# Diagonal 16x16 blocks of a chunk inverse moved from TensorE to GpSimd

## Chip, core and metric

The kernel runs on one core of one Trainium2 chip. The metric is device time in microseconds (us), from the first to the last instruction of a launch with what the device adds around it. PE is TensorE, PEld its weight loads, DVE is VectorE, ACT is ScalarE, POOL is GpSimd, SP is SyncE, which here only issues DMAs.

## What is computed

A delta rule attention (4 batches, 8 heads, 768 positions, head dimension 48) feeds a mixture of 8 experts that keeps at most 80 tokens of each expert (model dimension 384, hidden 1024). All in f32.

```python
for t in range(S):                                   # attention, per batch and head
    y[:, :, t] = einsum('bhd,bhde->bhe', q[:, :, t], state)
    v_old = einsum('bhde,bhd->bhe', state, kt)        # kt: normalised key
    state = state + bt * einsum('bhd,bhe->bhde', kt, vt - v_old)
...
expert_idx = argmax(x @ w_gate, axis=1)               # x: attention output, (3072, 384)
for e in range(8):
    tok_idx = the 80 tokens of expert e with the largest gate weight
    out[tok_idx] = gate_w[tok_idx, None] * (relu(x[tok_idx] @ w1[e]) @ w2[e])
```

## The kernel before

The sequence is cut into 12 chunks of 64 positions (`NC`, `C`). All 32 heads of a chunk are worked on at once: two halves `e` of the partitions times two `p` times eight `g`. A chunk has two parts. `prep(c)` (lines 304 to 377) doesn't need the state of earlier chunks: it transposes the keys and queries (L311, copied by ACT at L314), forms the two 64x64 Gram matrices (L319), scales and masks them into `B1` and `PT` (L324, L327, and POOL's affine selects at L330 and L332), and builds the inverse of the unit triangular 64x64 matrix `B1` of each head by six doublings: blocks of 2 come from the masks (L336, L340, L343), then five levels each multiply on PE (L353), mask on DVE (L357), multiply twice (L362 and L370) and copy on ACT (L366, L374). The result is `Y`. `chain(c)` (lines 384 to 448) is the recurrent part: state times keys and queries (L393, L398), `R` (L396), `Y` times `R` (L406), `U` (L409), the new state (L415, L419), the output rows `x` (L423, L428), which go to `x_rows` in DRAM (L433), and the gate logits (L439 to L447). `gate(b)` turns the logits of three chunks into expert choices and candidate lists (`cand`), mostly in small DVE instructions.

Each f32 matmul stands twice in the trace, as two instructions with a weight load each, so a group of 32 heads is 64 rows of PE; the 128x128 transposes stand once. One chunk has, by the loops of the code, 16 transposes (L311), 128 of L319, 64 of L340, 320 of L353, 256 of L362, 320 of L370, and 338 of the chain (five groups of 64, 6 of L439, 12 of L446): 1442.

`weave` alternates the steps of `chain(c)`, of the second half of `prep(c + 1)` and of the first half of `prep(c + 2)`; engines run their instructions in the order of one static list each. PSUM tiles of two banks (`mtile`) are used in turn, three of them. `norms(c)` is a square on ACT (L240), some twelve small DVE instructions, and one POOL multiply (L258).

Two of ten weight buffers are loaded early (`WR0 = 2`); the other eight loads stand right behind the chunk loop (L564 and L565), and behind them on SP the six loads of `mg` (L588), a gather of the candidate lists over partitions. Then a selection on DVE and PE finds the tokens (L593 to L647), POOL gathers them from `x_rows` (L659), and the experts run on PE (L683, L691).

Of the kernel before, what the change touches and what calls it, by code (L numbers as in the profile page):

```python
# [24 lines left out]
def kernel(  # L25
# [20 lines left out]

    nc = tc.nc
# [4 lines left out]
    C = 64  # L52
# [18 lines left out]

    const = ctx.enter_context(tc.tile_pool(name="const", bufs=1))
# [11 lines left out]
    eye = const.tile([128, 64], F32, name="eye")  # L84
    nc.gpsimd.memset(strict, 1.0)
    nc.gpsimd.memset(eye, 0.0)
    for e in range(2):
# [6 lines left out]
    widths = []  # L94
    w = 1
    while w < C:
        widths.append(w)
        w *= 2
    masks = []
    for w in widths:  # L100
        m = const.tile([128, 64], F32, name=f"mask{w}")
        nb = 64 // (2 * w)
        nc.gpsimd.memset(m, 0.0)
        for e in range(2):
            r = slice(64 * e, 64 * e + 64)
            lo = m[r].rearrange("p (g j) -> p g j", g=nb)[:, :, 0:w]
            nc.gpsimd.memset(lo, -1.0)
            nc.gpsimd.affine_select(out=lo, in_=lo, compare_op=Alu.is_ge, fill=0.0, base=-w,
                                    pattern=[[-2 * w, nb], [0, w]], channel_multiplier=1)
            nc.gpsimd.affine_select(out=lo, in_=lo, compare_op=Alu.is_ge, fill=0.0, base=2 * w - 1,  # L110
                                    pattern=[[2 * w, nb], [0, w]], channel_multiplier=-1)
        nc.gpsimd.tensor_tensor(out=m, in0=m, in1=eye, op=Alu.add)
        masks.append(m)
    mask1T = const.tile([128, 64], F32, name="mask1T")
    nc.gpsimd.memset(mask1T, 0.0)
    for e in range(2):
        r = slice(64 * e, 64 * e + 64)
        odd = mask1T[r].rearrange("p (g j) -> p g j", j=2)[:, :, 1:2]
        nc.gpsimd.memset(odd, -1.0)
        nc.gpsimd.affine_select(out=odd, in_=odd, compare_op=Alu.is_equal, fill=0.0, base=0,  # L120
                                pattern=[[-2, 32], [0, 1]], channel_multiplier=1)
    nc.gpsimd.tensor_tensor(out=mask1T, in0=mask1T, in1=eye, op=Alu.add)
# [25 lines left out]
    WR0, WR = 2, 10  # L148
    w_t, w_pools = {}, [wpool]

    def load_w(i):
# [4 lines left out]
        w_t[i] = w_pools[late].tile([128, nch, DK * F // nch], F32, name=f"w{i}", tag="w", bufs=WR - WR0 if late else WR0)  # L156
        nc.sync.dma_start(w_t[i], src[i // 2].rearrange("(c p) f -> p c f", p=128))

    with ExitStack() as actx:
# [13 lines left out]
        NKB, NQB = 4, 3  # L173
# [3 lines left out]
        def load_k(c):  # L177
            if c >= NC:
                return
            kr[c] = inp.tile([128, NB, D], F32, name="kr", bufs=4)  # L180
# [29 lines left out]
        for t in kn + qn:  # L210
            nc.vector.memset(t[:, :, D:], 0.0)
        load_q(0)
        load_k(1)
        load_v(0)
        load_q(1)
        load_k(2)
# [85 lines left out]
        Fs = {}  # L302

        def prep(c):
            kb, qb = kn[c % NKB], qn[c % NQB]
            KT = mat.tile([128, NQ, 128], F32, name="KT")
            QT = mat.tile([128, NQ, 128], F32, name="QT")
            for dst, src in ((KT, kb), (QT, qb)):
# [6 lines left out]
            yield  # L315
            pk, pq = mtile(), mtile()
            for ps, r in ((pk, KT), (pq, QT)):
# [4 lines left out]
            B1 = mat.tile([128, 2, NQ, 64], F32, name="B1")  # L322
            PT = mat.tile([128, 2, NQ, 64], F32, name="PT")
            halves(lambda s: nc.vector.tensor_tensor(  # L324
                out=B1[:, :, s], in0=sq4(pk)[:, :, s],
                in1=beta_t[:, c, :, s].unsqueeze(3).to_broadcast([128, 2, 4, 64]), op=Alu.mult))
            halves(lambda s: nc.vector.tensor_tensor(out=PT[:, :, s], in0=sq4(pq)[:, :, s], in1=wide(strict), op=Alu.mult))  # L327
            bv = B1.rearrange("r p g w -> r (p g) w")
            for e in range(2):
                nc.gpsimd.affine_select(out=bv[hs(e)], in_=bv[hs(e)], compare_op=Alu.is_gt, fill=0.0, base=0,  # L330
                                        pattern=[[0, 2 * NQ], [1, 64]], channel_multiplier=-1)
                nc.gpsimd.affine_select(out=bv[hs(e)], in_=bv[hs(e)], compare_op=Alu.not_equal, fill=1.0, base=0,  # L332
                                        pattern=[[0, 2 * NQ], [1, 64]], channel_multiplier=-1)
            yield
            Y = mat.tile([128, 2, NQ, 64], F32, name="Y")
            nc.gpsimd.tensor_tensor(out=Y.rearrange("r p g w -> r (p g) w"), in0=bv,  # L336
                                    in1=mask1T.unsqueeze(1).to_broadcast([128, 2 * NQ, 64]), op=Alu.mult)
            px = mtile()
            tiles(lambda e, p: (e, e),
                  lambda e, p, g: nc.tensor.matmul(px[hs(e), p, 64 * g : 64 * g + 64],  # L340
                                                   lhsT=B1[hs(e), p, g], rhs=eye[hs(e)], start=True, stop=True))
            X = mat.tile([128, 2, NQ, 64], F32, name="X", bufs=2)
# [380 lines left out]
```

## Time and profile before

| | us |
|---|---|
| median of three runs | 738.8 (735.47 to 745.18) |
| the profiled execution | 735.01 |
| its span, first to last instruction | 733.3 |
| PE busy | 505.5 (69%) |
| DVE busy | 297.4 (41%) |
| ACT busy | 174.5 (24%) |
| POOL busy | 140.8 (19%) |

Busy time is the time in which at least one instruction of the engine ran. Matmuls of different quadrants of the array overlap, so many instructions of 0.2 us fit in a busy microsecond. A wait named "issue" is idle time of an engine in which it waited for nothing that the profile shows.

### The profile page before, as it was taken

To read this page: it belongs to the slowest core of one execution; us is meant where nothing else is said; L and a number is where in the kernel's file an instruction comes from. 1 tells how busy PE (TensorE), PEld (TensorE's weight loads), DVE (VectorE), ACT (ScalarE), POOL (GpSimd) and SP (SyncE) were. 2 spreads that over 40 slices of the span, in tenths; PEclk is the share of its full clock that TensorE was granted. 3 is DMA by queue.
4 is the path that set the end of the run, shared out by engine and by line. 5 is a ranking of instruction groups with operands and counts; after the bars stand their busy time and mean duration, and the time that the engine had idled before them with its cause. 6 is when DMAs were issued, how large, how long until landed. Compare 5 with 4: busy or idle time off the path is not lost. (4 is left out here: it accounts for less than half of the span.)

```text
span 733.3 us, 37473 instructions
## 1 busy us (share of the span) xinstructions
PE 505.5 (69%) x17681; PEld 456.2 (62%) x17681; DVE 297.4 (41%) x745; ACT 174.5 (24%) x326; POOL 140.8 (19%) x198
## 2 busy tenths in 40 slices
PE   0567578767786685968878677786857200499997
PEld 0557568767785675958777576786757200377774
DVE  1575356234372446324433641443363617400000
ACT  0303432323333223231322314133222000000000
POOL 7180003040310402104131040312000200301000
PEclk9969989999899999998789999899999655589999
DMA  4994033120222202121120111100001890158200
GB/s 89 265 205 122 4 75 126 34 61 4 47 47 47 48 4 46 26 47 26 22 50 5 26 26 26 25 4 11 20 5 26 308 389 13 41 189 294 74 14 14
DMA packets 94154, 53.26 MB, mean 73 GB/s; under 512 B 77616, under 2 KB 88880, under 8 KB 94000
## 3 DMA queue, kind: packets, MB, share of 16 engines
q1 hardware_dynamic: 92064, 48.78, 24.8%
q8 instruction: 139, 2.28, 1.3%
q0 software_dynamic: 768, 1.97, 0.9%
q10 hardware_dynamic: 1168, 0.11, 0.1%
q14 instruction: 15, 0.12, 0.1%
HBM read 40.42 MB, written 10.42 MB: 69 GB/s over the span
## 5 line engine op out<-in xcount | busy, mean ns | idle before, releaser
L357 DVE TENSOR_TENSOR P<-pm,mask 128x512 f32<-128x512 f32 x120 | 77.1, 684 | 111.8 <-PE pm L353 111.7
L353 PE MATMUL pm<-X,B 64*64 64x64 f32 x3840 | 93.9, 230 | 28.4 <-issue 28.4
L366 ACT COPY X<-pm 128x512 f32<-128x512 f32 x96 | 51.5, 589 | 232.3 <-PE pm L362 232.3
L353 PEld LDWEIGHTS pm<-X,B 64*64 64x64 f32 x3840 | 83.8, 143 | 32.5 <-issue 32.3
L370 PE MATMUL pm<-Y,P 64*64 64x64 f32 x3840 | 87.4, 223 | 20.1 <-issue 18.3
L370 PEld LDWEIGHTS pm<-Y,P 64*64 64x64 f32 x3840 | 79.7, 138 | 23.0 <-issue 22.9
L362 PE MATMUL pm<-P,Y 64*64 64x64 f32 x3072 | 76.6, 228 | 23.6 <-DVE P L357 11.2
L362 PEld LDWEIGHTS pm<-P,Y 64*64 64x64 f32 x3072 | 69.5, 141 | 29.0 <-issue 22.9
L330 POOL TENSOR_SCALAR_AFFINE_SELECT B<-B 64x1024 f32<-64x1024 f32 x24 | 27.5, 1147 | 287.1 <-DVE B L324 276.9
L374 ACT COPY Y<-pm 128x512 f32<-128x512 f32 x120 | 64.7, 595 | 38.9 <-PE pm L370 38.9
L683 PEld LDWEIGHTS hp<-xTe,w 128*128 128x128 f32 x384 | 49.0, 210 | 2.1 <-issue 1.2
L683 PE MATMUL hp<-xTe,w 128*128 128x80 f32 x384 | 48.8, 292 | 0.0
L691 PE MATMUL yp<-w,hT 128*80 128x384 f32 x128 | 43.4, 493 | 0.0
L686 ACT ACTIVATE hT<-hp 128x320 f32<-128x320 f32 x16 | 7.0, 438 | 149.6 <-issue 75.8
L340 PE MATMUL pm<-eye,B 64*64 64x64 f32 x768 | 32.9, 249 | 9.7 <-POOL B L332 5.7
L340 PEld LDWEIGHTS pm<-eye,B 64*64 64x64 f32 x768 | 30.8, 163 | 11.2 <-POOL B L332 8.5
L324 DVE TENSOR_TENSOR B<-pm,beta_t 128x512 f32<-128x512 f32 x24 | 15.4, 686 | 40.3 <-PE pm L319 40.3
L691 PEld LDWEIGHTS yp<-w,hT 128*80 128x80 f32 x128 | 18.9, 153 | 19.8 <-issue 19.8
L336 POOL TENSOR_TENSOR Y<-B,mask1T 128x1024 f32<-128x1024 f32 x12 | 28.3, 2362 | 0.3
L258 POOL TENSOR_TENSOR kn<-kr,inv 128x768 f32<-128x768 f32 x12 | 17.7, 1478 | 54.8 <-PE S_ps L415 38.7
L601 PE MATMUL tb_ps<-ident,thrw 8*128 8x8 f32 x1 | 0.2, 239 | 40.4 <-DVE thrw L599 40.4
L332 POOL TENSOR_SCALAR_AFFINE_SELECT B<-B 64x1024 f32<-64x1024 f32 x24 | 27.5, 1147 | 1.6
(156 smaller groups left out, 644.9 us busy)
## 6 DMA issues: line engine op xcount, KB each, us to landing
w<-in_moe_w_dram SPq DMA_DIRECT2D x16, 1536.0 KB
kr<-in_k_dram SPq DMA_DIRECT2D x24, 192.0 KB
qn<-in_q_dram SPq DMA_DIRECT2D x24, 192.0 KB
vin<-in_v_dram SPq DMA_DIRECT2D x48, 96.0 KB
out_dram<-zero SPq DMA_DIRECT2D x12, 384.0 KB
x_rows<-x SPq DMA_DIRECT2D x24, 192.0 KB
bt<-in_beta_dram ACTq DMA_DIRECT2D x32, 3.0 KB
xg<-x_rows,idx_g POOLq DMA_INDIRECT x8, 2.7
```

What stands on the lines that cost most here:

```text
L330: nc.gpsimd.affine_select(out=bv[hs(e)], in_=bv[hs(e)], compare_op=Alu.is_gt, fill=0.0, base=0, pattern=[[0, 2 * NQ], [1, 64]], channel_mu ...
L332: nc.gpsimd.affine_select(out=bv[hs(e)], in_=bv[hs(e)], compare_op=Alu.not_equal, fill=1.0, base=0, pattern=[[0, 2 * NQ], [1, 64]], channe ...
L336: nc.gpsimd.tensor_tensor(out=Y.rearrange("r p g w -> r (p g) w"), in0=bv, in1=mask1T.unsqueeze(1).to_broadcast([128, 2 * NQ, 64]), op=Alu ...
L340: lambda e, p, g: nc.tensor.matmul(px[hs(e), p, 64 * g : 64 * g + 64], lhsT=B1[hs(e), p, g], rhs=eye[hs(e)], start=True, stop=True))
L353: lambda e, p, g: nc.tensor.matmul(pp[hs(f(e, p)), pb(e, p), 64 * g : 64 * g + 64], lhsT=B1[hs(e), p, g], rhs=X[hs(e), xb(e, p), g], start ...
L357: halves(lambda s: nc.vector.tensor_tensor(out=P2[:, :, s], in0=sq4(pp)[:, :, s], in1=wide(masks[n]), op=Alu.mult))
L362: lambda e, p, g: nc.tensor.matmul(px[hs(e), xo(e, p), 64 * g : 64 * g + 64], lhsT=Y[hs(f(e, p)), yb(e, p), g], rhs=P2[hs(f(e, p)), pb(e, ...
L366: halves(lambda s: nc.scalar.copy(X[:, :, s], sq4(px)[:, :, s]))
L370: lambda e, p, g: nc.tensor.matmul(py[hs(yh(e, p)), yo(e, p), 64 * g : 64 * g + 64], lhsT=P2[hs(f(e, p)), pb(e, p), g], rhs=Y[hs(f(e, p)), ...
L374: halves(lambda s: nc.scalar.copy(Y[:, :, s], sq4(py)[:, :, s]))
L683: nc.tensor.matmul(hp[:, (f - f0) * cap : (f - f0 + 1) * cap], lhsT=w1_t[:, c, f * 128 : (f + 1) * 128], rhs=xTs[e][:, c, :], start=(c == ...
L691: nc.tensor.matmul(yp[:cap, :DM], lhsT=hT[:, f, :], rhs=w2_t[:, f, :], start=(f == 0), stop=(f == FK - 1))
```

## The change

The doubling now starts at blocks of 16. The four diagonal 16x16 blocks of each of the 32 heads are 128 small triangular systems. After `gram(c)` two DMAs write `B1` to a DRAM scratch, one DMA reads the 128 diagonal blocks back with one block per partition (`NT`), POOL inverts them by 14 steps of two instructions (`solve`), one DMA writes the 128 inverses to DRAM, and eight DMAs read them back into the block diagonal of `xe`. PE then makes the two upper merges, 16 to 32 and 32 to 64 (`merge`). `B1` gets its sign and strict triangle from a precomputed product of beta and a mask (`bm`, one POOL multiply of 128x1024), so POOL's affine selects and the multiply at L336 go. `weave` is replaced by a written order over four chunks in flight: in turn c the chain of c, the merge of c+1, the solve of c+2, and the transposes and Gram matrices of c+3. All ten weight loads now stand behind the loads of `mg`. The copy at L441 moves from DVE to ACT. Buffers of `qn` go from three to two, of `kr` from four to three.

```diff
+    PB = 16 * 65
+    a_dram = [nc.dram_tensor(f"a_blocks{i}", (128 * PB,), F32, kind="Internal") for i in range(2)]
+    i_dram = [nc.dram_tensor(f"inv_blocks{i}", (128, 256), F32, kind="Internal") for i in range(2)]
...
-    WR0, WR = 2, 10
+    WR0, WR = 0, 10
...
+        def scale(c):
+            if c >= NC:
+                return
+            norms(c)
+            bm = mat.tile([128, 2, NQ, 64], F32, name="bm", bufs=1)
+            nc.gpsimd.tensor_tensor(out=bm.rearrange("r p g w -> r (p g) w"),
+                                    in0=beta_t[:, c].rearrange("r p g -> r (p g)").unsqueeze(2).to_broadcast([128, NB, 64]),
+                                    in1=neg_strict.unsqueeze(1).to_broadcast([128, NB, 64]), op=Alu.mult)
+            bms[c] = bm
...
+            halves(lambda s: nc.vector.tensor_tensor(out=B1[:, :, s], in0=sq4(pk)[:, :, s], in1=bm[:, :, s], op=Alu.mult))
             halves(lambda s: nc.vector.tensor_tensor(out=PT[:, :, s], in0=sq4(pq)[:, :, s], in1=wide(strict), op=Alu.mult))
...
+            ad = a_dram[c % 2]
             for e in range(2):
+                dst = ad.rearrange("(e g z) -> e g z", e=2, g=NB)[e, :, : 64 * 64].rearrange("g (r w) -> r g w", w=64)
+                nc.sync.dma_start(dst, B1[hs(e)].rearrange("r p g w -> r (p g) w"))
+            NT = NTs[c] = sml.tile([128, 16, 16], F32, name="NT")
+            nc.sync.dma_start(NT, ad.rearrange("(s z) -> s z", z=PB)[:, :1024].rearrange("s (r w) -> s r w", w=64)[:, :, :16])
+
+        def solve(c):
+            if c >= NC:
+                return
+            NT = NTs.pop(c)
+            X = sml.tile([128, 16, 16], F32, name="Xs")
+            nc.gpsimd.tensor_tensor(out=X, in0=NT.rearrange("p s t -> p t s"), in1=eye16, op=Alu.add)
+            for t in range(14, 0, -1):
+                sh = [128, 15 - t, t]
+                tmp = sml.tile([128, 64], F32, name="tmp")
+                tv = tmp[:, : (15 - t) * t].rearrange("p (c s) -> p c s", s=t)
+                nc.gpsimd.tensor_tensor(out=tv, in0=X[:, t + 1 :, t : t + 1].to_broadcast(sh),
+                                        in1=NT[:, 0:t, t].unsqueeze(1).to_broadcast(sh), op=Alu.mult)
+                nc.gpsimd.tensor_tensor(out=X[:, t + 1 :, 0:t], in0=X[:, t + 1 :, 0:t], in1=tv, op=Alu.add)
+            nc.sync.dma_start(i_dram[c % 2][:, :], X.rearrange("p c s -> p (c s)"))
+            src = i_dram[c % 2].rearrange("(e g i) (c s) -> e i c g s", e=2, i=4, s=16)
+            dst = xe[c % 2].rearrange("r p g w -> r (p g) w")
+            for e in range(2):
+                for i in range(4):
+                    nc.sync.dma_start(dst[64 * e + 16 * i : 64 * e + 16 * i + 16, :, 16 * i : 16 * i + 16], src[e, i])
+
+        def merge(c):
...
+            X, B1 = xe[c % 2], B1s.pop(c)
+            py, pp = mtile(), mtile()
+            tiles(lambda e, p: (e, p),
+                  lambda e, p, g: nc.tensor.matmul(py[hs(p), e, 64 * g : 64 * g + 64], lhsT=X[hs(e), p, g], rhs=eye[hs(e)],
+                                                   start=True, stop=True))
...
+            for n in range(2):
+                nc.tensor.matmul(pp[:, n, :], lhsT=identb, rhs=eyes.rearrange("r g w -> r (g w)"), start=True, stop=False,
+                                 skip_group_check=True)
...
-            nc.vector.tensor_copy(xT, pt[:, :, : DK * 128].rearrange("r b (j w) -> r b j w", w=128))
+            nc.scalar.copy(xT, pt[:, :, : DK * 128].rearrange("r b (j w) -> r b j w", w=128))
...
-            weave(*gens)
+            load_k(c + 4)
+            load_v(c + 2)
+            ch, mg = chain(c), merge(c + 1)
+            if c > 0:
+                step(ch)
+            if c + 3 < NC:
+                trans(c + 3)
+            load_q(c + 4)
+            step(ch)
+            step(mg)
+            step(ch)
+            if c + 3 < NC:
+                gram(c + 3)
+            solve(c + 2)
+            scale(c + 4)
+            step(mg)
+            step(ch)
+            step(mg)
+            step(ch)
+            step(mg)
...
-    for i in range(WR0, WR):
-        load_w(i)
...
         for t in range(NT):
             nc.sync.dma_start(mg[:, t, :], last[t * E : (t + 1) * E, :CW])
+        for i in range(WR0, WR):
+            load_w(i)
```

The merge of a chunk is six groups of 64 instructions on PE (a transpose of `X` by the identity, `B1` times `X`, then two products of the first merge, one of 32x32 blocks, and one that gives `Y`) and the two bf16 matmuls of 512 columns that add the identity: 386. A turn with all four chunks in flight has 338 + 16 + 128 + 386 = 868.

## Rows read from the trace of the kernel before

**Rows 1.** The page: its head line.

```profile
span 733.3 us, 37473 instructions
```

**Rows 2.** Busy time by stretch: eleven chunks; us, PE, PEld, DVE, ACT, POOL, clock, DMA share.

```profile
119.60:575.10 455.50, 342.05 (x14725) 321.51 (x14716) 191.26 (x456) 136.40 (x256) 80.85 (x80) 0.94 0.14 30
```

**Rows 3.** Same stretch, one line alone each: L311, L340, L439, L446; PE, PEld.

```profile
119.60:575.10 455.50, 20.74 (x144) 18.16 (x144) 0.94 0.14 30
119.60:575.10 455.50, 22.31 (x576) 21.16 (x576) 0.94 0.14 30
119.60:575.10 455.50, 9.59 (x66) 7.01 (x66) 0.94 0.14 30
119.60:575.10 455.50, 17.08 (x132) 16.08 (x132) 0.94 0.14 30
```

**Rows 4.** Waits of PE in that stretch: us in total, times, longest.

```profile
PE pm L353 <- issue: 23.3, 21, 2.0
...
PE pm L362 <- DVE P L357: 9.4, 11, 0.9
```

**Rows 5.** Timeline of PE, 225 to 239 us: start, us, instructions, idle before them.

```profile
225.82 0.50 PE L393 MATMUL pm<-st,KT 48*64 48x48 f32 x19 [1.75 <-issue]
...
229.49 0.57 PE L353 MATMUL pm<-X,B 64*64 64x64 f32 x23 [1.58 <-issue]
...
235.23 0.85 PE L362 MATMUL pm<-P,Y 64*64 64x64 f32 x41 [1.83 <-issue]
...
238.95 0.85 PE L319 MATMUL pm<-KT 48*64 48x64 f32 x41 [1.63 <-issue]
```

**Rows 6.** The page: one DMA queue; packets, MB, share of 16 engines.

```profile
q8 instruction: 139, 2.28, 1.3%
```

**Rows 7.** Groups by line, POOL: busy us, mean ns of one, idle before.

```profile
L336 POOL TENSOR_TENSOR Y<-B,mask1T 128x1024 f32<-128x1024 f32 x12 | 28.3, 2362 | 0.3
...
L258 POOL TENSOR_TENSOR kn<-kr,inv 128x768 f32<-128x768 f32 x12 | 17.7, 1478 | 54.8 <-PE S_ps L415 38.7 <-DVE inv L257 9.1 <-DVE nt L249 6.3
...
L490 POOL TENSOR_SCALAR rhs<-oh,pp 128x48 bf16<-128x48 f32 x4 | 2.1, 518 | 0.0
...
L496 POOL TENSOR_TENSOR rest<-rest,rhs 128x48 f32<-128x48 f32 x4 | 1.2, 294 | 0.3
```

**Rows 8.** Timeline, 36 us: one POOL pair and a DVE instruction beside it.

```profile
36.04 2.38 POOL L330 TENSOR_SCALAR_AFFINE_SELECT B<-B 64x1024 f32<-64x1024 f32 x2 [7.87 <-DVE seed L244]
36.08 1.12 DVE L248 SCALAR_TENSOR_TENSOR nt<-ss,seed 128x16 f32<-128x16 f32 x1
```

**Rows 9.** Timeline of SP and ACT: DMA issues, and a square that waits for one.

```profile
107.67 1.39 SPq L183 DMA_DIRECT2D kr<-in_k_dram  x2
...
114.06 0.84 ACT L240 ACTIVATE sq<-kr 128x768 f32<-128x768 f32 x1 [6.82 <-DMA kr<-in_k_dram]
...
451.71 2.65 SPq L200 DMA_DIRECT2D vin<-in_v_dram  x4
```

**Rows 10.** Instructions that touch `x_rows`: DMA from issue to landing.

```profile
DMA to landing us min/median/max: 2.7/2.7/3.0
```

**Rows 11.** Timeline before the loop: first transposes, and the chain's first matmuls.

```profile
25.52 1.97 PE L311 MATMUL pm<-ident,kn 128*128 128x128 f32 x8 [7.23 <-POOL kn L258]
...
96.38 1.17 PE L406 MATMUL pm<-vin,Y 64*64 64x48 f32 x64 [0.73 <-ACT Y L374]
```

**Rows 12.** Timeline behind the loop: last logits, weight and `mg` loads, first selection.

```profile
575.07 0.17 DVE L447 COPY lg<-pm 128x16 f32<-128x16 f32 x1 [2.12 <-PE pm L446]
...
592.47 9.06 SPq L588 DMA_DIRECT2D mg<-cand  x6
...
607.57 0.65 DVE L593 MAX8 top<-mg 8x8 f32<-8x480 f32 x1 [17.39 <-DMA mg<-cand]
```

**Rows 13.** Busy time by stretch: a DMA-bound one, and one of low clock.

```profile
195.00:201.00 6.00, 5.00 (x207) 4.85 (x202) 1.69 (x4) 0.86 (x2) 5.72 (x6) 0.50 0.03 5
...
580.00:590.00 10.00, 0.38 (x1) 0.11 (x1) 8.65 (x34) 0.00 (x0) 1.53 (x5) 0.50 1.05 391
```

More of the change, by code (lines that the diff above doesn't have):

```diff
@@ L92 @@
                                 pattern=[[1, 64]], channel_multiplier=-1)
[L94 to L122, printed above, removed]
+        lo = mask[r].rearrange("p (g j) -> p g j", g=2)[:, :, 0:16]
@@ new lines @@
+        nc.gpsimd.memset(lo, 1.0)
+        nc.gpsimd.affine_select(out=lo, in_=lo, compare_op=Alu.is_ge, fill=0.0, base=-16,
+                                pattern=[[-32, 2], [0, 16]], channel_multiplier=1)
+        nc.gpsimd.affine_select(out=lo, in_=lo, compare_op=Alu.is_ge, fill=0.0, base=31,
+                                pattern=[[32, 2], [0, 16]], channel_multiplier=-1)
+    nc.gpsimd.tensor_tensor(out=mask, in0=mask, in1=eye, op=Alu.add)
+    neg_strict = const.tile([128, 64], F32, name="neg_strict")
@@ new lines @@
+    nc.gpsimd.tensor_scalar(neg_strict, strict, -1.0, None, op0=Alu.mult)
+    identb = const.tile([128, 128], BF16, name="identb")
+    nc.gpsimd.tensor_copy(identb, ident)
+    eyes = const.tile([128, NQ, 64], BF16, name="eyes")
+    nc.gpsimd.tensor_copy(eyes, eye.unsqueeze(1).to_broadcast([128, NQ, 64]))
+    eye16 = const.tile([128, 16, 16], F32, name="eye16")
+    nc.gpsimd.memset(eye16, 0.0)
+    nc.gpsimd.affine_select(out=eye16, in_=eye16, compare_op=Alu.not_equal, fill=1.0, base=0,
+                            pattern=[[1, 16], [-1, 16]], channel_multiplier=0)
@@ L321, in prep @@
                                                        start=True, stop=True))
[L322 to L326, printed above, removed]
+            B1 = B1s[c] = mat.tile([128, 2, NQ, 64], F32, name="B1")
+            PT = PTs[c] = mat.tile([128, 2, NQ, 64], F32, name="PT")
@@ L334, in prep @@
-            yield
[L335 to L341, printed above, removed]
@@ L516, in zeros, with step @@
                 nc.sync.dma_start(zr[i], zero)
-        def weave(*gens):
-            live = list(gens)
-            while live:
-                for g in list(live):
-                    if next(g, live) is live:
-                        live.remove(g)
-        def steps(g, n):
-            for _ in range(n):
-                if next(g, g) is g:
-                    return
-                yield
-        NSTG = 14
-        HALF = 7
-        norms(0)
-        norms(1)
-        preps = {0: prep(0), 1: prep(1)}
-        weave(steps(preps[0], NSTG), steps(preps[1], HALF))
-        for i in range(WR0):
-            load_w(i)
+        def step(g):
+            next(g, None)
+        scale(0)
+        load_k(2)
+        trans(0)
+        gram(0)
+        scale(1)
+        load_k(3)
+        load_q(2)
+        solve(0)
+        trans(1)
+        gram(1)
+        scale(2)
+        load_q(3)
+        load_v(1)
+        solve(1)
+        for _ in merge(0):
+            pass
+        trans(2)
+        gram(2)
+        scale(3)
         gates = iter(())
         for c in range(NC):
-            load_k(c + 3)
-            load_q(c + 2)
-            load_v(c + 1)
-            norms(c + 2)
-            gens = [chain(c)]
-            if c + 1 < NC:
-                gens.append(preps.pop(c + 1))
-            if c + 2 < NC:
-                preps[c + 2] = prep(c + 2)
-                gens.append(steps(preps[c + 2], HALF))
-            weave(*gens)
+            load_k(c + 4)
[18 more added lines that the diff above has]
+            step(mg)
             zeros(c)
```

120 lines of the change are left out of this document (62 added, 58 removed).

## The prediction

> **What bounds the kernel now.** First the head of the page and its stages: the chunk loop from the chain's first matmuls to the last logits is 575.1 - 96.4 = 478.7 us of a span of 733.3 [rows 1, 11, 12], so the loop decides. Then busy time over eleven chunks, 119.6 to 575.1: 455.5 / 11 = 41.4 us a chunk, of which PE is busy 31.1, DVE 17.4, ACT 12.4 and POOL 7.35 [rows 2]. PE is the engine to look at, and it is idle 10.3 us a chunk. The waits say what that idle time is: the largest wait on another engine is 9.4 us in all of the stretch, for the masked product of L357, while the groups that ended with "issue" are led by L353 alone with 23.3 [rows 4]. So PE is seldom late for data. The timeline shows a pattern in it: PE stops at 225.82, 229.49, 235.23 and 238.95 for 1.6 to 1.8 us each, and from the first of these restarts to the next I count 127 matmuls [rows 5]. The instruction queue moved 2.28 MB in 139 packets for 37473 instructions [rows 1, 6]: 61 bytes each and 16.4 KB a packet, about 270 instructions, close to 127 matmuls with their weight loads (254). So PE stops once per packet of its instructions, and in the steady loop it costs (455.5 - 342.05) / (14725 / 128) = 113.5 / 115 = 0.99 us per 128 matmuls, the few data waits included [rows 2]. The loop is bound by the number of PE instructions, partly through execution and partly through their supply.
>
> The Trainium skill speaks against this reading: Runtime: NRT & Kernel Launch, section Instruction fetch mechanics, says that a 16 KiB block boundary costs one tail bump that is mostly hidden. The stops at block distance in this trace disagree [rows 5]. By the page the 10.3 us of idle time would not come from the count of instructions and would stay; that is the second rival below.
>
> **The change, part by part.** *PE.* A turn falls from 1442 to 868 instructions (both counted from the loops). Cost of one turn: 16 transposes at 20.74 / 144 = 0.144 us, 2.3; 6 of L439 at 0.145, 0.9; 12 of L446 at 0.129, 1.55 [rows 3]. The two bf16 matmuls of 512 columns move 1024 columns, as eight transposes do: 1.15, taken between nothing and that of L446's twelve. The other 832: in the stretch all lines but those four are busy 342.05 - 69.72 = 272.3 us for 14725 - 918 = 13807 instructions, 19.7 ns each [rows 2, 3]; 832 x 19.7 ns = 16.4. (L340, which uses two of the four quadrants at 22.31 / 576 = 38.7 ns, disappears; the transposes of `X` that stand in its place use all four.) Busy 22.3 us. Stops: 868 / 128 x 0.99 = 6.7. One turn: 29.0 us instead of 41.4. The busy share stays at 77% against 75% now, so I leave the clock at the 0.94 of the stretch.
>
> *POOL.* Its affine selects and the multiply of L336 go. It gets `bm`, of L336's shape, 2.36 us, and keeps L258, 1.48 [rows 7]. The solve is 28 small instructions over 1120 elements per partition in all and one over 256. From 294 ns at 48 elements and 2362 at 1024 one element costs 2.12 ns and the fixed part 192 ns [rows 7]: 28 x 0.192 + 1120 x 2.12 ns = 7.8, plus 0.7. For steps between dependent instructions I add 0.1 us each, an estimate, 2.8. Solve: 11.3 us; below, 5.4 of fixed parts alone; above, every instruction at the 518 ns of L490, 14.5 + 3.5 = 18.0. I take 11.3, since L496 is the same operation. POOL: 15.1 us a turn (at most 21.9), under 29.
>
> *DVE and ACT* lose four of five masked products, L343 and L441, and half of the copies of X and Y, against a few copies that come in; both start under 17.4 us a turn and stay under it [rows 2]. A small DVE instruction took 1.12 us while a POOL pair ran [rows 8], so DVE will be held up by POOL: some 30 small ones a turn (norms, gate) times one POOL instruction of 0.28 is 8.4 us, hidden as DVE stays below 26.
>
> *DMA.* Each turn gains 12 DMAs on SP (two stores of `B1`, `NT`, the store of the inverses, eight of `xe`) beside 10 for k, v, q, and x rows; 22 x 0.66 us of issue [rows 9] is 14.5, under 29. Landing after the last issue: 2.7 us [rows 10]; above, the k load that was issued at 107.67 and used at 114.06, 6.4 [rows 9]; none is below 2.7 in these rows. I take 2.7, as these DMAs are small too. What must be in time: SP works in order, and in the written order the inverses of c+2 are stored behind the `NT` load of c+3, which waits for the landing of `B1`. So from `B1` of c+3 to `xe` of c+2: 1.3 + 2.7, 0.66, 0.66 + 2.7, 8 x 0.66 + 2.7 = 16.0 us. There is time from the end of the key Gram matrix (530 of 868 instructions into the turn) to the first product of the merge in the next turn (208 in): 0.63 of a turn, 18.3 us at 29.0, less 1.4 for `B1` itself on DVE. That holds by less than 1 us; with the upper landing it is 27 us and doesn't. Behind SP's wait stand also the zeros and the loads of k and v of the next turn; they are needed a whole turn later.
>
> *Before the loop.* The first transposes stay at 25.5 [rows 11]. From there: transposes and Gram 7, `B1` 1.3, store and `NT` 4 + 3.4, solve 11.3, store and `xe` 3.4 + 8, merge of four groups of steps with a copy behind each, about 16: the chain starts at 80 instead of 96.4 (68 with nothing for the steps, 95 with the upper prices).
>
> *Behind the loop.* The first selection waits 17.4 us for `mg`, whose six loads were issued from 592.47 on, behind the weights [rows 12]. Ahead of them, six issues at 0.66 and a landing make 6.7: 10.7 us saved, 0 to 14.7. The ten weight loads then run 15.7 MB at 391 GB/s [rows 13], 40 us, into the gather of the tokens; I take 2 back for it. Two weight loads leave the start, where nothing on the path waited for them.
>
> *Sum.* After the chain starts there are 740 instructions in the first turn, eight turns of 868, two of 724 and one of 274: 9406, that is 10.84 turns. 80 + 10.84 x 29.0 = 394, 3.5 for the last chain, which runs alone, and from the last logits to the end 733.3 - 575.1 - 8.7 = 149.5: span 547, and with the 1.7 us that the profiled execution has around its span 549. That execution, 735.0, is 0.5% below the median of 738.8, which I leave in the rounding: 545 to 550. In general: time = 235 + 10.84 x turn.
>
> **Rivals.** 1. *The supply alone is the limit.* Between two restarts 127 matmuls took 3.67 us [rows 5]; if execution hides under that, a turn is 868 / 127 x 3.67 = 25.1 and the time 507. For it: the spacing repeats as 3.72 at the end of rows 5. Against it: the piece between, with transposes in it, took 5.74.
>
> 2. *The idle time is not the supply but waits that the profile doesn't show.* Then 10.3 us stay: 22.3 + 10.3 = 32.6, time 588. A lower clock gives much the same: at 0.50, the level of 1.2 GHz, 207 instructions took 5.0 us [rows 13], 24 ns for 19.7, so 3.7 us a turn more, 589.
>
> 3. *POOL becomes the bound.* The Trainium skill, GPSIMD Engine Reference, section When to use GPSIMD, sends elementwise work to VectorE, and its specifications say the two share their SBUF interface. The blocked DVE instruction agrees [rows 8]. Worked from rows: if each small instruction costs as much as the 1.12 us that one engine held up the other, the solve is 28 x 1.12 + 3.5 = 35, POOL 39 us a turn, and the time 658. Against it: L496 ran at 294 ns on this engine.
>
> 4. *The other side: SP's order makes the trips serial.* The turn is then the trip and the 1.4 over 0.63. At 27 us of trip it is 45 and the time 723, within some 2% of now; from 29 us of trip on, when each of the three landings takes 7.0 us, it is over 48 and the kernel is slower. For it: a landing of 6.4 was seen beside five other transfers, and each trip has packets of 64 bytes, which the trace doesn't show. Against it: DMA was busy 0.14 of the loop [rows 2], and SP's list need not keep the written order.
>
> **How the numbers follow.** The likeliest case is the sum, turns of 27 to 31 us, 528 to 571: 0.55. Supply alone, 500 to 528: 0.14. Idle or clock, or a trip a little too long, 571 to 615: 0.18. POOL or SP between, 615 to 720: 0.07. The serial trip: 0.06, of it 0.03 within 2% and 0.03 slower. Some 2% is what a measurement tells from no change here. Leaving out what lies above 605 and below 500 gives the range 500 to 605. Faster 0.94, same 0.03, slower 0.03.
>
> **What the new profile would show.** PE's matmuls fall to about 10,800 by the counts; the stops stand again at every 128 of them. If the step from count to time is right, the last logits of neighbouring turns are 27 to 31 us apart and PE stays over 70% busy. POOL's small instructions should take 0.2 to 0.35 us. PE should not wait for DMA into `xe`, nor ACT for k. `mg` should land some 7 us after `cand`. I am wrong if PE's first wait is for `xe` or for POOL, if SP's largest wait is the landing of `B1`, or if the turns keep near 41 us with fewer instructions.

## The result and the profile after

The changed kernel takes 563.4 us (median of four runs, 559.2 to 565.8) against 741.3 us of the kernel before, a ratio of 0.760 with an interval from 0.752 to 0.767. Medians here are of all runs of a kernel, while ratios leave out the runs that are over 1.5% slower than its fastest. The forecast was 547, its range 500 to 605. The profiled execution took 562.0 us, its span 560.3.

The page of the kernel after: the head line, busy time of the engines, two DMA queues (packets, MB, share), and groups by line (busy us, mean ns of one, idle before).

```profile
span 560.3 us, 23721 instructions
...
PE 385.1 (69%) x10793; PEld 334.5 (60%) x10793; DVE 227.2 (41%) x624; ACT 122.0 (22%) x218; POOL 177.7 (32%) x461
...
q1 hardware_dynamic: 169632, 59.80, 44.4%
...
q8 instruction: 85, 1.39, 1.0%
...
L355 POOL TENSOR_TENSOR tmp<-Xs,NT 128x14 f32<-128x14 f32 (+6 forms) x168 | 47.8, 284 | 13.0
...
L408 PE MATMUL pm<-Y,p 64*64 64x64 f32 x768 | 45.8, 298 | 2.0 <-DVE p L404 1.3
...
L309 POOL TENSOR_TENSOR bm<-beta_t,neg_strict 128x1024 f32<-128x1024 f32 x12 | 22.9, 1908 | 59.4 <-DVE rn L244 35.0
```

PE has 10,793 matmuls, as counted. The instruction queue moved 85 packets instead of 139 [rows 6], of the same 16.4 KB. PE's matmuls and weight loads alone are 2 x 10,793 / 85 = 254 to a packet, and 2 x 17,681 / 139 = 254 before: the 270 of the prediction counted the instructions of all engines. PE's busy share of the span is unchanged at 69%.

Busy time by stretch, over seven turns with all four chunks in flight (last logits at 139.5 to last logits at 345.3); columns as in [rows 2]. Then L408 and L376 alone in it (the block product that gives `Y`, and the two bf16 products).

```profile
139.50:345.30 205.80, 166.91 (x6079) 153.25 (x6080) 106.34 (x287) 66.55 (x118) 84.54 (x229) 0.83 0.51 99
...
139.50:345.30 205.80, 26.62 (x449) 24.34 (x450) 0.83 0.51 99
139.50:345.30 205.80, 4.24 (x14) 0.79 (x14) 0.83 0.51 99
```

A turn is 205.8 / 7 = 29.4 us: PE busy 23.84, idle 5.56, DVE 15.2, ACT 9.5, POOL 12.1. The mean granted clock is 0.83, where it was 0.94 before [rows 2]. What PE waited for in that stretch (us in total, times, longest):

```profile
PE pm L330 <- issue: 12.9, 7, 2.4
PE S_ps L450 <- DVE U L444: 6.8, 7, 1.9
PE pm L391 <- issue: 5.5, 4, 2.7
```

There is no wait for `xe` in the loop. The timeline of PE in one turn (start, us, instructions, idle before) shows the stops:

```profile
182.52 0.98 PE L371 MATMUL pm<-eye,xe 64*64 64x64 f32 x51 [0.32 <-issue]
...
186.52 1.16 PE L330 MATMUL pm<-KT 48*64 48x64 f32 x50 [1.87 <-issue]
...
190.12 1.60 PE L386 MATMUL pm<-P,Y 64*64 64x32 f32 x51 [0.45 <-issue]
```

From the first of these restarts to the second I count 128 matmuls in 4.00 us, from the second to the third 127 in 3.60. In the third the stop is only 0.45 us, because execution took longer there: from about 187.5 on PE ran at a granted clock of 0.50, the level of 1.2 GHz.

Behind the loop: the last logits, the loads of `mg`, and the first selection with its wait.

```profile
410.94 0.17 DVE L482 COPY lg<-pm 128x16 f32<-128x16 f32 x1 [5.31 <-PE pm L481]
...
425.61 4.21 SPq L631 DMA_DIRECT2D mg<-cand  x6
...
431.10 0.65 DVE L638 MAX8 top<-mg 8x8 f32<-8x480 f32 x1 [5.05 <-DMA mg<-cand]
```

The chain's first matmul is at 84.78 us. So the span is 84.8 + 326.1 + 149.4, where the forecast had 80 + 317.9 + 149.5.

### The profile page after: what moved, and what is told of

It is laid out like the page before. It is cut to its first block, busy times and chain, and to the rows that moved or that the text cites. A ratio compares the mean times of both kernels' runs of the same rounds, so it can differ in the third digit from the quotient of the medians.

```text
span 560.3 us, 23721 instructions
## 1 busy us (share of the span) xinstructions
PE 385.1 (69%) x10793; PEld 334.5 (60%) x10793; DVE 227.2 (41%) x624; ACT 122.0 (22%) x218; POOL 177.7 (32%) x461
## 5 line engine op out<-in xcount | busy, mean ns | idle before, releaser
L355 POOL TENSOR_TENSOR tmp<-Xs,NT 128x14 f32<-128x14 f32 (+6 forms) x168 | 47.8, 284 | 13.0
L357 POOL TENSOR_TENSOR Xs<-Xs,tmp 128x14 f32<-128x14 f32 (+6 forms) x168 | 44.9, 267 | 12.9
L408 PE MATMUL pm<-Y,p 64*64 64x64 f32 x768 | 45.8, 298 | 2.0 <-DVE p L404 1.3
L408 PEld LDWEIGHTS pm<-Y,p 64*64 64x64 f32 x768 | 41.9, 208 | 3.6 <-DVE p L404 2.2
L371 PE MATMUL pm<-eye,xe 64*64 64x64 f32 x768 | 19.9, 237 | 30.4 <-DMA xe<-inv_blocks 25.5
L371 PEld LDWEIGHTS pm<-eye,xe 64*64 64x64 f32 x768 | 16.9, 148 | 31.6 <-issue 28.2
L481 PE MATMUL pm<-wg,xT 128*128 128x8 f32 x144 | 27.3, 323 | 2.6 <-ACT xT L476 2.0
L391 PE MATMUL pm<-Y,P 64*64 64x64 f32 x768 | 20.8, 260 | 11.7 <-issue 11.7
L411 ACT COPY Y<-pm 128x512 f32<-128x512 f32 x24 | 12.9, 589 | 72.0 <-PE pm L408 72.0
L481 PEld LDWEIGHTS pm<-wg,xT 128*128 128x128 f32 x144 | 26.2, 278 | 3.9 <-ACT xT L476 2.9
L382 DVE TENSOR_TENSOR P<-pm,mask 128x512 f32<-128x512 f32 x24 | 15.4, 683 | 30.7 <-PE pm L379 30.7
L391 PEld LDWEIGHTS pm<-Y,P 64*64 64x64 f32 x768 | 18.3, 171 | 12.8 <-issue 12.8
```

The costliest lines, as they stand in the source:

```text
L355: nc.gpsimd.tensor_tensor(out=tv, in0=X[:, t + 1 :, t : t + 1].to_broadcast(sh), in1=NT[:, 0:t, t].unsqueeze(1).to_broadcast(sh), op=Alu.mult)
L357: nc.gpsimd.tensor_tensor(out=X[:, t + 1 :, 0:t], in0=X[:, t + 1 :, 0:t], in1=tv, op=Alu.add)
L371: lambda e, p, g: nc.tensor.matmul(py[hs(p), e, 64 * g : 64 * g + 64], lhsT=X[hs(e), p, g], rhs=eye[hs(e)], start=True, stop=True))
L382: halves(lambda s: nc.vector.tensor_tensor(out=P2[:, :, s], in0=sq4(pp)[:, :, s], in1=wide(mask), op=Alu.mult))
L391: lambda e, p, g: nc.tensor.matmul(py[hs(e ^ p), p, 64 * g : 64 * g + 64], lhsT=P2[hs(p), e, g], rhs=Y16[hs(p), e, g], start=True, stop=True))
L408: lambda e, p, g: nc.tensor.matmul(py[hs(e ^ p), p, 64 * g : 64 * g + 64], lhsT=P5[hs(e ^ p), e, g], rhs=Y4[hs(e ^ p), p, g], start=True, ...
```

## Experiments

The theory: the turn is set by the number of PE instructions, and the trip through DRAM with POOL's solve is hidden in the loop. The rivals: the trip, POOL or the DMA traffic still costs time in the loop; or the turn is PE's execution alone, without a floor from the supply of instructions. In the table, "instr." are PE instructions in a full turn, "idle" is PE's, and the clock is the mean granted one of the stretch; all by busy time in a stretch of six or seven full turns of the profiled execution.

| kernel | instr. | turn | PE busy | idle | clock | total |
|---|---|---|---|---|---|---|
| changed kernel | 868 | 29.4 | 23.8 | 5.6 | 0.83 | 563.4 |
| the same, again | 868 | 30.2 | 23.4 | 6.8 | 0.85 | 567.0 |
| a third time, in the last series | 868 | 30.6 | 24.3 | 6.4 | 0.81 | 561.6 |
| e1_quad | 868 | 30.5 | 23.7 | 6.9 | 0.81 | 560.5 |
| e2_slow_solve | 868 | 29.7 | 23.6 | 6.1 | 0.84 | 591.7 |
| e3_no_trip | 868 | 29.5 | 23.6 | 5.9 | 0.81 | 535.8 |
| e5_pad_small | 1124 | 37.8 | 28.7 | 9.1 | 0.73 | 653.2 |
| e6_pad_big | 880 | 30.7 | 23.8 | 6.9 | 0.95 | 579.4 |
| e9_quad_y16_dma | 804 | 32.0 | 25.3 | 6.7 | 0.70 | 578.3 |
| e10_loads_on_act | 804 | 27.8 | 21.7 | 6.2 | 0.82 | 567.7 |
| e11_loop_loads_on_act | 804 | 29.8 | 23.5 | 6.4 | 0.75 | 571.0 |

**The changed kernel again.**

> The changed kernel once more, as the common measure of the other runs on this chip: 563 us within 0.7%, a ratio of 0.76 to the kernel before. No theory is told apart by it.

567.0 us (559.8 to 569.3). Three profiles of this one program (the third is from the last series) have turns of 29.4, 30.2 and 30.6 us; below, a difference under 1.2 us in a turn alone is not read as an effect, and totals decide.

**The solve made slower.** The multiply of each of the 14 steps three times:

```diff
+                for _ in range(3):
-                nc.gpsimd.tensor_tensor(out=tv, in0=X[:, t + 1 :, t : t + 1].to_broadcast(sh),
+                    nc.gpsimd.tensor_tensor(out=tv, in0=X[:, t + 1 :, t : t + 1].to_broadcast(sh),
```

> Each of the 14 multiplies of the solve is issued three times instead of once: 28 more POOL instructions of 0.29 us, with 0.09 between them some 10.5 us a chunk; POOL busy 12.1 + 8 = 20 us of a turn of 29.4. Theory A (the trip is hidden): the turn stays within 0.5 us; only the first chunk, which nothing covers, is later by 10.5, so 563 + 10 = 573. Theory C (POOL or the trip is on the path): 10.5 us in each of twelve turns, about 680.

591.7 us (589.9 to 592.2), ratio 0.796 (0.790 to 0.802). The stretch of seven turns, the largest wait of PE in the whole span, and one of its parts in the timeline:

```profile
166.70:374.50 207.80, 164.99 (x6080) 151.31 (x6080) 99.17 (x287) 66.24 (x118) 142.44 (x430) 0.84 0.50 100
...
PE pm L372 <- DMA xe<-inv_blocks: 47.4, 6, 36.2
...
146.95 0.45 PE L372 MATMUL pm<-eye,xe 64*64 64x64 f32 x2 [4.92 <-DMA xe<-inv_blocks]
```

POOL rises to 142.44 / 7 = 20.3 us a turn and the turn stays at 29.7. The first logits come at 132.5 instead of 110.4: the solves of the first two chunks have nothing to hide behind, 2 x 10.5 = 21. That, with the 4.9 us at 146.95 in which PE waits for the third, is 27 of the 28 us by which the total rose; the 573 expected allowed for one solve. POOL is not the bound. But 10.5 us more use up about all the room that the trip has: PE waits for `xe` 1.6 us in the seven turns, and 4.5 in the last ones.

**The solve and the trip left out.** `solve` does nothing, the stores of `B1` and the load of `NT` go, and `xe` holds identities, so the diagonal blocks of the inverse are left out:

```diff
-        for t in xe:
-            nc.gpsimd.memset(t, 0.0)
-        for t in p5:
+        for t in xe + p5:
...
-            NT = NTs.pop(c)
+            return
```

> Left out: the solve on POOL and its twelve DMAs per chunk (two stores of B1, the load of NT, the store of the inverses, eight loads of xe); xe holds identities instead, so the inverse is wrong. PE, DVE and ACT do the same work. Theory A: the chain starts some 28 us earlier (no store, load, solve, store and load ahead of the first merge), the turn stays within 0.7 us of 29.4: 563 - 28 = 535, down to 525 if freed DMA engines shorten the stops. Theory C (the trip sets the turn): the turn falls to PE's own 24 to 25 us, the kernel to 480. If the traffic of 64-byte packets is what makes the stops, PE's idle time falls from 5.6 to under 3 us a turn, about 505.

535.8 us (532.4 to 538.0), ratio 0.720 (0.713 to 0.727).

```profile
117.30:323.60 206.30, 165.23 (x6080) 152.56 (x6080) 89.60 (x260) 64.19 (x115) 24.87 (x26) 0.81 0.24 52
```

POOL falls to 3.6 us a turn, the DMA share from 0.51 to 0.24, and the turn is 29.5. PE is idle 5.9 us as before. So neither the trip nor the traffic of small packets nor POOL costs anything in the loop, and the traffic doesn't make PE's stops. The trip costs its length once: the first logits come at 86.1 instead of 110.4, 24 of the 28 us.

**More instructions, little work.** 256 products of 8 columns (128 matmuls, each standing twice) ahead of the 32x32 product of each merge:

```diff
+            for _ in range(4):
+                tiles(lambda e, p: (e, e ^ p),
+                      lambda e, p, g: nc.tensor.matmul(pp[64 * (e ^ p) + 32 : 64 * (e ^ p) + 64, e, 64 * g : 64 * g + 8],
...
```

> The changed kernel with 256 needless PE instructions more in each merge, four groups of 32x32 products with 8 columns, ahead of L398 and overwritten by it; a turn has 1124 instructions instead of 868, two blocks of 128 more. At 11 to 13 ns each they execute in some 3 us. Theory A (execution and stops add up, 0.82 us for each block): 3 + 1.6 = 4.6 us a turn, 12 merges: 567 + 55 = 622. Theory B (a block takes as long as its supply, 3.6 us, when it executes faster than that): two blocks at 3.6 us, 7.2 us a turn, 567 + 86 = 653, and PE's idle time grows by 4 us a turn. Rival D (the idle time has nothing to do with the count): 3 us a turn of busy time, idle time unchanged, 603.

653.2 us (648.2 to 655.4), ratio 0.877 (0.872 to 0.883). The stretch, the added products (L399) alone in it, PE's first wait there, and two of its stops in the timeline:

```profile
161.20:425.60 264.40, 200.81 (x7871) 185.73 (x7872) 105.14 (x287) 66.55 (x118) 78.10 (x211) 0.73 0.40 79
161.20:425.60 264.40, 25.08 (x1792) 23.20 (x1792) 0.73 0.40 79
...
PE pm L399 <- issue: 21.8, 12, 3.3
...
228.00 1.82 PE L399 MATMUL pm<-X,B 32*32 32x8 f32 x122 [3.32 <-issue]
...
231.45 1.06 PE L403 MATMUL pm<-X,B 32*32 32x32 f32 x59 [1.52 <-issue]
```

The added products are busy 25.08 / 7 = 3.6 us a turn. By the totals they cost (653.2 - 563.4) / 12 = 7.5 us a merge, 3.7 for each 128 instructions (7.2 and 7.6 by the other two medians of the changed kernel; by the turns 8.4, 7.6 and 7.1); PE's waits for them are for nothing that the profile shows. From the restart at 228.00 to the one at 231.45, 128 matmuls took 3.45 us though they execute in less than 2. So a block of 128 matmuls takes its supply time even if there is next to nothing to execute. That the total is the 653 of the supply theory is in part luck. The clock fell to 0.73 in the same run, and PE's other work was busy 28.7 - 3.6 = 25.1 us a turn, 0.8 to 1.7 more than in the three profiles of the changed kernel; the idle time grew by 2.3 to 3.5, where the theory had 4.

**More work, few instructions.** Twelve bf16 products of 512 columns in the same place:

```diff
+            for n in range(12):
+                nc.tensor.matmul(pp[:, n % 2, :], lhsT=identb, rhs=eyes.rearrange("r g w -> r (g w)"), start=True, stop=True)
```

> The changed kernel with twelve needless bf16 products of 512 columns more in each merge, at the same place and overwritten too: a turn has 880 instructions. At the 0.30 us that L376 takes they execute in 3.6 us, as much as the padding of the other run. Theory A: 3.6 us a turn and hardly a stop more, 567 + 44 = 611. Theory B (long instructions give the supply time): part of the idle time of 5.6 us goes under them, some 1.5 us; 2.1 us a turn, 592. If the granted clock (0.83 in the loop) rises because the array is kept busy, lines that stood at half clock gain up to 4 us a turn and nearly nothing is lost: 570.

579.4 us (577.6 to 582.1), ratio 0.779 (0.776 to 0.782). The stretch, the twelve products (L398) and the block product that is L408 in the changed kernel (L410 here):

```profile
146.00:360.60 214.60, 166.54 (x6164) 141.21 (x6163) 102.07 (x288) 66.50 (x118) 81.74 (x224) 0.95 0.48 95
146.00:360.60 214.60, 20.63 (x84) 8.71 (x84) 0.95 0.48 95
...
146.00:360.60 214.60, 16.82 (x450) 14.90 (x449) 0.95 0.48 95
```

Work of 20.63 / 7 = 2.9 us cost (579.4 - 563.4) / 12 = 1.3 us a merge by the totals (1.0 and 1.5 by the other two medians) and left PE's busy time where it was, because everything else ran faster: the granted clock is 0.95 instead of 0.83, and the block product takes 16.82 instead of 26.62 us. The time lies between the 592 of the supply theory without a change of clock and the 570 with one. What the clock costs the changed kernel can be read off: without the twelve, PE is busy (166.54 - 20.63) / 7 = 20.8 us at 0.95 and 23.8 at 0.83, so 3.0 us a turn (2.6 and 3.4 by the other two profiles of the changed kernel).

**The block product on four quadrants.** L408 uses two of the array's four quadrants, (e^p, e^p). Keeping the first merge in the half e^p spreads it over all:

```diff
-            tiles(lambda e, p: (e, p),
-                  lambda e, p, g: nc.tensor.matmul(pp[hs(p), e, 64 * g : 64 * g + 64], lhsT=B1[hs(e), p, g], rhs=X[hs(e), p, g],
+            tiles(lambda e, p: (e, e ^ p),
+                  lambda e, p, g: nc.tensor.matmul(pp[hs(e ^ p), e, 64 * g : 64 * g + 64], lhsT=B1[hs(e), p, g], rhs=X[hs(e), p, g],
...
-            tiles(lambda e, p: (e ^ p, e ^ p),
+            tiles(lambda e, p: (p, e ^ p),
```

> The first merge is kept in the half e^p instead of p, so that the last product of the merge (L408) runs on all four 64x64 quadrants of the array instead of two; counts and work are otherwise the same. Theory A (PE execution and the stops at each block of instructions add up): L408 falls from 3.80 us a turn to about 1.9, the level of L391, the turn from 29.4 to 27.5, the kernel by 12 x 1.9 = 23 us to 540. Theory B (the supply of instructions alone sets the turn): the stops grow by what L408 gives back, the turn stays at 29.4 and the kernel at 563. Theory C (the trip over DRAM sets the turn): PE waits for xe, no gain, 563.

560.5 us (556.6 to 563.7), ratio 0.753 (0.745 to 0.761): no difference that can be told from the three medians of the changed kernel, 561.6 to 567.0. The stretch, and the block product alone:

```profile
136.20:349.90 213.70, 165.70 (x6079) 150.53 (x6079) 105.35 (x287) 66.93 (x118) 84.17 (x229) 0.81 0.49 96
136.20:349.90 213.70, 16.57 (x449) 14.05 (x449) 0.81 0.49 96
```

The product itself fell from 26.62 to 16.57 us, 1.4 us a turn of the 1.9 expected, and PE's busy time hardly did: other lines got longer (the transposes L320 from 13.76 to 16.98, L428 from 12.44 to 15.37, L481 from 14.91 to 17.83 in seven turns; the other two profiles of the changed kernel have 13.76, at most 13.73 and at most 15.91) at a clock of 0.81. The gain of one line came back as a cost of the others; that the clock is the reason is read from these rows and wasn't tried by itself.

**The loads of `mg` first, alone, in the kernel before.** The eight late weight loads go behind `mg`, and nothing else changes:

```diff
-    for i in range(WR0, WR):
-        load_w(i)
...
             nc.sync.dma_start(mg[:, t, :], last[t * E : (t + 1) * E, :CW])
+        for i in range(WR0, WR):
+            load_w(i)
```

> The kernel before, with one part of the change alone: the loads of mg stand ahead of the eight late weight loads. Theory A (that part of the change is worth what the sum gave it): the wait of the first selection falls from 17.4 to about 5 to 7 us, the gather of the tokens loses 2 to 3 of it to the weights, the kernel gets 8 to 10 us faster, a ratio of 0.988. Rival: the time of the weights only moves, and the first expert waits for its gather or its weights; no change, 1.00.

734.8 us (723.5 to 738.2) against 744.0 on the same chip, ratio 0.979 (0.971 to 0.988). This ratio rests on two of the four runs; the medians give 0.988. The last logits, the issue of `mg` and the first selection (before: [rows 12]):

```profile
588.51 0.17 DVE L447 COPY lg<-pm 128x16 f32<-128x16 f32 x1 [2.82 <-PE pm L446]
...
603.18 4.21 SPq L586 DMA_DIRECT2D mg<-cand  x6
608.56 0.65 DVE L593 MAX8 top<-mg 8x8 f32<-8x480 f32 x1 [4.95 <-DMA mg<-cand]
```

The wait is 4.95 instead of 17.39 us, and from the last logits to the end of the span it is 735.4 - 588.5 = 146.9 us instead of 158.2. So the order was worth 11.3 us there, where 8 to 10 were expected; the two ratios make 9 and 16 us of it.

**64 instructions fewer.** The products of `X` with the identity (L371) can go: POOL makes a turned copy `XT`, four DMAs store it and eight load it as `ye`. With the merge of the kernel after:

```diff
+            nc.gpsimd.tensor_copy(XT, X.rearrange("p c s -> p s c"))
...
+                    nc.sync.dma_start(into[64 * h + 16 * i : 64 * h + 16 * i + 16, :, 16 * i : 16 * i + 16], turned[h, i])
...
-            tiles(lambda e, p: (e, p),
-                  lambda e, p, g: nc.tensor.matmul(py[hs(p), e, 64 * g : 64 * g + 64], lhsT=X[hs(e), p, g], rhs=eye[hs(e)],
-                                                   start=True, stop=True))
```

> The transposed inverse is no longer made by 64 products with the identity on PE; POOL makes a turned copy and 12 more DMAs (four stores, eight loads) put it in place. Theory A (the number of PE instructions sets the turn): 64 instructions fewer a turn, 10.88 / 7 = 1.55 us of PE and half a stop, 0.41: turn 27.5 instead of 29.4, total 563 - 11 x 1.96 + 3 (the first trip gets longer) = 544. Theory C (part is given back by the granted clock, as it seemed when the first merge was spread over four quadrants, where 16 us became 6): about 553. Theory D (SP's list, now 34 issues or some 22 us a turn, and the longer trip are late for the merge): 575 or more, with a PE wait for the DMA into ye.

592.0 us (586.4 to 601.3), ratio 0.789 (0.783 to 0.796). And with the merge of e1_quad:

> The turned copy by DMA and the first merge kept in the half that lets the 32x32 product run on four quadrants, together. Theory A: 544 less 11 x 1.43 us of L408 = 528. Theory C (the granted clock gives part of both back): 545. Theory D: 565 or more, with a PE wait for the DMA into ye.

578.3 us (577.0 to 581.1), ratio 0.774 (0.769 to 0.780). Both are slower than the changed kernel, and not for the reason written down: PE waits for `ye` once, 2.0 and 1.4 us, ahead of the loop. A wait of PE in six turns of e9 (140.9 to 332.8), and SP's wait for the solve in its whole span:

```profile
PE pm L322 <- POOL kn L252: 6.0, 5, 2.3
...
SPq L362 <- POOL Xs L359: 73.7, 11, 16.2
```

PE now waits in the loop for the normalised keys, 1 us a turn. SP waits for the solve 73.7 us in all, and the loads of k are in its list behind that; the DVE and POOL steps that make the keys end just ahead of the transposes that need them. The larger part of the loss is PE's busy time, 25.3 us a turn with fewer instructions, at a clock of 0.70.

So the loop's loads were put on ACT's queue, first all of them, then only those inside the loop (e9 is the base of both):

```diff
-                nc.sync.dma_start(kr[c][64 * e : 64 * e + 64], src[e, c])
+                nc.scalar.dma_start(kr[c][64 * e : 64 * e + 64], src[e, c])
```

> As the run with the turned copy by DMA and the first merge over four quadrants, with the loads of k, v and q issued by ACT instead of SP. Theory E (there PE waited for the normalised keys, 6 to 19 us in six turns, and lost the rest to a granted clock of 0.70, because the loads of k stood in SP's list behind the wait for the solve): the keys are early again, turn 27.5 at the clock of 0.81 to 0.83 that the other runs had, total 535 to 550. Theory F (the lost time comes from the 12 DMAs of the turned copy themselves, or from the lower clock that a lighter PE load brings with it): as there, about 578. Eight issues more on ACT, some 5 us a turn beside 8 of work, should cost nothing in either.

567.7 us (565.0 to 570.4), ratio 0.768 (0.764 to 0.772). PE no longer waits for the normalised keys in the loop, as theory E had it, and the turn is what the count of instructions promised:

```profile
156.80:351.60 194.80, 151.69 (x5631) 137.00 (x5632) 91.21 (x259) 55.94 (x101) 87.49 (x236) 0.82 0.49 86
```

27.8 us a turn against the expected 27.5, at 0.82. But the first logits come at 124.9 instead of 110.4, and that takes most of the gain: ACT issues the 32 loads of beta and the first loads of k, q and v one behind the other (beta from 2.3 to 20.8 us, with the loads of the first k ahead of it, not behind sixteen of beta as the next expectation has it), and its first square starts at 31.1 instead of 17.6.

> As the run before, but with the loads ahead of the loop on SP again and only the loop's loads of k, v and q on ACT. Theory E: in the run before a turn took 27.8 us and the first logits came 14.5 us late (124.9 against 110.4), because the first loads stood on ACT behind the sixteen loads of beta; the turn stays at 27.8, the first logits come at about 110, total about 553, 10 under the changed kernel. Theory G (the lower turn came from the other instruction order that the late start gave): the turn goes back to 29 or more, total 565 or more.

571.0 us (568.2 to 575.6), ratio 0.770 (0.764 to 0.776); the changed kernel in the same series:

> The changed kernel on the same chip, for the comparison with the run before: 563.

561.6 us (559.7 to 567.2), ratio 0.758 (0.752 to 0.763). The start is back (first logits at 113.4), and the turn is 29.8:

```profile
148.10:356.90 208.80, 164.30 (x5631) 149.33 (x5631) 90.72 (x259) 56.69 (x101) 87.44 (x236) 0.75 0.52 100
```

With the same instructions in the loop as the run before, PE is busy 164.30 / 7 = 23.5 us a turn at 0.75, there 21.7 at 0.82. PE also waits 1.8 us for `ye` and 3.0 for a masked product that stands behind the trip. Busy time times mean clock is the same in e9, e10 and e11: 25.3 x 0.70, 21.7 x 0.82 and 23.5 x 0.75 are 17.6 to 17.8. So the difference in busy time is the clock's. What set the clock apart, the order of the lists or something else, stays open, and with it whether 27.8 can be had again. No version that computes the right result beat the changed kernel.

## Why the prediction was right

**The bound.** It stands. Stops come every 127 or 128 matmuls in the kernel after too; idle time per 128 is (205.80 - 166.91) / (6079 / 128) = 0.82 us, in the other two profiles 1.00 and 0.94, forecast 0.99; 6.8 of the 38.9 us are the wait for `U` in the list above. The first half of the second rival, that the 10.3 us of idle time have nothing to do with the number of instructions, would have left them; 5.6 to 6.8 are left. The 7.5 us for 256 nearly empty instructions in e5 say it directly. The Trainium skill's sentence in Runtime: NRT & Kernel Launch, section Instruction fetch mechanics, that a block boundary is mostly hidden, doesn't hold for these runs: a stop of 1.87 us stands in the timeline above, and blocks with little in them took 3.45 us. It comes near only where execution covers most of the supply, as at the stop of 0.45.

A better form of my term seems to be that each block of 128 takes the longer of its execution and some 3.6 us. It fits e5, but not all of [rows 5]. There the block from 229.49 to 235.23 executed for 3.9 us without a break, and PE still stood for 1.83. Busy time by stretch in the kernel before; then the instruction queue in three short windows, 232.4 to 232.5 of the kernel before, 184.1 to 184.2 and 187.6 to 187.7 of the kernel after (packets, MB, share):

```profile
229.49:233.40 3.91, 3.91 (x126) 3.53 (x126) 1.58 (x3) 2.05 (x4) 0.00 (x0) 1.00 0.44 84
233.40:235.23 1.83, 0.00 (x1) 0.00 (x1) 0.73 (x2) 0.00 (x0) 0.00 (x0) 1.00 0.62 115
...
q8 instruction: 1, 0.02, 82.2%
...
q8 instruction: 1, 0.02, 59.9%
q8 instruction: 1, 0.02, 70.4%
```

Each of these packets is the only one that starts between two restarts, and PE restarts 2.4 to 2.8 us behind it, at 235.23, 186.52 and 190.12. So the stops are waits for the next packet. It starts 1.1 to 3.0 us behind the restart of its block, latest where sixteen transposes stand near the block's head; what makes it start isn't shown. Some 3.5 us are a floor for a block, and where its long instructions stand counts too. The first rival, supply alone with 25.1 us a turn, fell because the blocks of a turn take 29.4 / (868 / 128) = 4.3 us on average: those with transposes and gate products, and those at the lower clock, take longer than the floor.

**The turn: right by terms that offset each other.** 29.4 for 29.0, which is closer than the terms deserve. Three were off. First, the clock: I left it at 0.94 because the busy share stayed; it came out at 0.83, and by e6's stretch that costs 3.0 us a turn. This is the lower-clock rival, realised in part and hidden by the other two. Second, PE's terms together were too dear by about 1.5 for a clock of 0.94: PE at 0.95 in e6 is busy 20.8 us without the added products, where I had 22.3. Within this, the step that failed outright, the other way, is L408: I priced its 64 instructions at 1.26 us like those that use four quadrants, though I had seen that L340 on two of them costs twice as much [rows 3]. It takes 3.80 us, of which 16.82 / 7 - 1.26 = 1.1 are, as an estimate, the quadrants (e6's clock) and 1.4 the clock. The two bf16 products, priced at 1.15, took 4.24 / 7 = 0.6. Third, the stops: 5.6 instead of 6.7 in this profile (6.8 and 6.4 in the other two); a stop that slower execution covers in part is the one of 0.45 above.

**POOL.** 28 small instructions took 214 to 327 ns each (median 296 for the multiplies), with some 0.09 us between dependent ones: 0.84 and then 47.75 to 57.53 in the first solve, 10.7 us; I had 11.3. `bm` took 1.91 us, not 2.36. POOL is busy 12.1 us a turn. The third rival (658) and with it the preference of the Trainium skill's GPSIMD Engine Reference, section When to use GPSIMD, for VectorE doesn't decide here: the slow engine is off the path, and in e2 10.5 us more on it moved the turn by less than two profiles of one kernel differ. DVE is held up as forecast (one small instruction of L241 took 1.89 us beside a `bm` of 1.90) and stays at 15.2 us.

**The trip.** Hidden, with more room than I gave it. Timeline of SP in one turn of the kernel after:

```profile
159.33 1.29 SPq L341 DMA_DIRECT2D a_blocks<-B  x2
160.72 2.02 SPq L358 DMA_DIRECT2D inv_blocks<-Xs  x1
...
164.68 0.37 SPq L343 DMA_DIRECT2D NT<-a_blocks  x1
165.16 6.09 SPq L363 DMA_DIRECT2D xe<-inv_blocks  x8
```

SP's list doesn't keep the written order: the inverses of c+2 are stored ahead of the `NT` load of c+3, so the two waits don't add up, and the last load of `xe` is issued some 9 us before the first use at 180.03. The landing of `B1` took at most 4.1 us from the end of its issue (the load of `NT`, which waits for it, starts at 164.68), where I had 2.7; with the written order 4.1 would have used up the margin that I computed. e3 shows that in the loop the trip is worth nothing. The serial rival (723 and up) had no part in it. SP's largest wait is for the rows of `x`, 59.8 us in ten, and hinders nobody.

**Before and behind the loop.** Timeline of PE at the start, the first product of the first merge and the first of the chain:

```profile
62.67 0.45 PE L371 MATMUL pm<-eye,xe 64*64 64x64 f32 x2 [25.52 <-DMA xe<-inv_blocks]
...
84.78 1.15 PE L441 MATMUL pm<-vin,Y 64*64 64x48 f32 x64
```

The chain starts at 84.8, forecast 80; the solve and its landings leave PE idle for 25.5 us, and e2 and e3 show that this stretch pays for the trip at full length. It is PE's only wait for `xe`, second in the span to 28.1 us in the selection, and the sum had it. In the loop there is none, so the sign of being wrong that I named, a first wait for `xe`, isn't there. The last three turns took 65.6 us, forecast 61.0. Behind the last logits 149.4 for 149.5: the first selection waited 5.05 us for `mg` (I had 6.7), and the gather of the tokens gave back 2.9 us (7.90 us ahead of the first `xp` instead of 5.0; I had 2). The sum of the parts is +4.8, +8.2 and -0.1 us of span against the forecast.

## What to carry to other kernels

Count PE's instructions before its work: where they are short, 128 f32 matmuls have a floor of some 3.5 us here whatever they compute, and 40% fewer instructions were worth 29% of a turn. Work moved to a slow engine through DRAM costs its whole length once, at the start, and nothing in the loop as long as the order gives it a turn of its own and the trip fits in it; extra DMAs on the same queue can still delay a load that has nothing to do with them. Don't carry PE's granted clock over from the kernel before, and don't expect a saving in one line of PE to reach the time in full.

## What was not expected of the hardware

The granted clock fell and rose within a turn. In the changed kernel one turn ran from 175 to 187 us at 1.00 (2.4 GHz) and from 188 to 194 at 0.50 (1.2 GHz); both rows are busy time by stretch.

```profile
175.00:187.00 12.00, 9.13 (x411) 8.12 (x406) 5.14 (x13) 5.58 (x11) 8.18 (x27) 1.00 0.47 93
188.00:194.00 6.00, 5.55 (x185) 5.29 (x178) 5.72 (x15) 0.91 (x2) 2.95 (x6) 0.50 0.52 118
```

In the six us before 188 PE had run groups of short products and stood still for 1.87 us. Adding twelve wide bf16 products to a turn raised the mean from 0.83 to 0.95, adding 256 narrow ones lowered it to 0.73, and taking 64 away came with 0.70 to 0.82. So 2.9 us of added work cost 1.0 to 1.5. Busy time times mean clock is nearly the same wherever PE's loop does the same work (19.1 to 19.9 us a turn in the three profiles of the changed kernel, e2 and e3, 17.6 to 17.8 in e9 to e11), so what differs in busy time between such runs is for the most part the clock. What the chip goes by isn't shown by these runs.
